# Seven products in place of eight for the first product of experts 3 to 7, with their weights through one staging buffer

## The chip, the cores and the metric

The kernel runs on one core of a Trainium2 chip. The metric is the time of one execution on the device, in microseconds (us); lower is better. The engines are PE (TensorE: matmuls, which write to PSUM, and PEld, its weight loads), DVE (VectorE), ACT (ScalarE), POOL (GpSimd) and SP (SyncE, which in the kernel before issues every DMA). Each engine runs its instructions in the order in which they stand in its queue; an instruction that waits for a semaphore holds up all that stand behind it.

## The reference

Gated linear attention makes 3072 rows of 384 values, and a mixture of eight experts works on every row with weights from a Sinkhorn iteration.

```python
# attention, batch 4, 8 heads, 768 steps, head dim 48
state = alpha[:, :, t, :, None] * state + einsum('bhd,bhe->bhde', k[:, :, t], v[:, :, t])
y[:, :, t] = einsum('bhd,bhde->bhe', q[:, :, t], state)

# experts: x [3072, 384], w_gate [384, 8], w1 [8, 384, 1024], w2 [8, 1024, 384]
P = exp(logits - logits.max())                  # logits = x @ w_gate
for _ in range(8):
    P /= P.sum(1, keepdims=True) + 1e-09
    P /= P.sum(0, keepdims=True) + 1e-09
    P *= N / E
for e in range(E):
    h = maximum(x @ w1[e], 0.0)
    out += P[:, e:e + 1] * (h @ w2[e])
```

## The kernel before, in words

Each operand of the experts' products is held as two float16 halves, high and low, and a product is made in three passes (high by high, high by low, low by high: `PASSES`). The rows come as `xT[0]` and `xT[1]`, with the 384 values in three k tiles of 128 partitions and 3072 tokens along the free axis. The weights are scaled by a power of two that comes from their largest entry, and split into `w1h` and `w2h`.

The program has three stages. In the first the attention runs, and the products of experts 0 and 1 fill TensorE between its steps (`filler`, `fill`). The second is the Sinkhorn iteration (`sinkhorn`): eight rounds in which DVE normalises rows, PE sums columns with one matmul (`pssk`), and DVE normalises columns. Between two rounds `fill(2.8)` puts about 2.8 us of the left-over products of experts 0 and 1 on PE. Up to there (`hold`) every engine's instructions stand in the order of the code. In the third stage, experts 2 to 7, PE keeps the order of the code and a scheduler places the instructions of the other engines when the program is built.

An expert is worked on in six tiles of 512 tokens (`moe_tile`). For each of eight f tiles, nine matmuls of 512 columns (three k tiles by three passes) add up in one PSUM bank. ACT then writes the relu as `h[0]`, and DVE writes what the rounding left as `h[1]`. For each of four groups of 128 tokens, 24 matmuls of 384 columns make the second product (tiles `ps2_...`), and DVE adds it to `acc` by `evac_add`. The PSUM banks come from a pool of four, `psm`; the other four belong to the attention's pools `psa` and `psb`.

`load_expert` brings the weights: one DMA of 1536 KB each for `w1f` and `w2f`, issued by SP into a pool `wst` of two buffers; three DVE maxima (`w1m`, `w2m`); a maximum over partitions on POOL (`w1g`, `w2g`); four small DVE steps (`pow2_scale`, steps m, p, r, s); and the split, ACT for the high half and DVE for the low. The split weights `wp` are double-buffered too. In the third stage one step of the next expert's load goes with every piece of this expert's products (`next(more, None)`), so that it lies all along the expert. Every instruction that a `Held` wrapper records is on line 56, every matmul on line 65.

Of the kernel before, what the change touches and what calls it, by code (L numbers as in the profile page):

```python
# [8 lines left out]
F16 = mybir.dt.float16  # L9
F32 = mybir.dt.float32  # L10
# [13 lines left out]
def tile_gla_moe(ctx: ExitStack, tc: tile.TileContext, q, k, v, alpha, wg, w1, w2, out):  # L24
# [21 lines left out]
    class Held:  # L46
        """an engine whose instructions stay in program order while hold is set"""
# [16 lines left out]
    def mm(out_, lhsT, rhs, start=True, stop=True):  # L64
        tc.keep_in_program_order(nc.tensor.matmul(out_, lhsT, rhs, start=start, stop=stop))  # L65
# [13 lines left out]
    mask = cp.tile([P, 8], F32, name="mask")          # mask[p, b] = (p // 16 == b)  # L79
# [158 lines left out]
    def attn_block(b, u, got):  # L238
        """scores inside blocks of 16 tokens; a partition is a (block, head)"""
# [67 lines left out]
        if fast:  # L307
# [111 lines left out]
    def attn_chunk(b, ch, got):  # L419
        """128 tokens; yields where its products wait for other engines"""  # L420
# [17 lines left out]
        def decayed(x, eng, tab, L, z, s):  # L438
            """the z-th halves of x's blocks of 2L, each block of 16 times its entry of tab"""
# [18 lines left out]
        # A^T [s, (h, t)], its blocks on the diagonal first  # L458
# [5 lines left out]
        # heads of one half of the partitions to a bank of their own  # L464
# [26 lines left out]
        # the scale of a token, and the token scaled  # L491
# [66 lines left out]
    w0, w1_ = (load_expert(e, None, wAB[e]) for e in range(2))  # L558
# [22 lines left out]
    def act(a):  # L581
        """a step of: the blocks of unit 1 or 2 (b), an expert's weights (w), a chunk (c), the gate (g), the experts (f)"""
# [53 lines left out]
    def sinkhorn():  # L636
# [7 lines left out]
        for it in range(N_SINKHORN):  # L644
# [11 lines left out]
            # (sum + EPS) * E / N, so that its inverse scales too  # L656
# [5 lines left out]

    ws, wn = [], []
# [10 lines left out]
    hold[0] = False  # L674

# [21 lines left out]

    for e in range(2, E):
        wn = []
        more = load_expert(e + 1, wst, wn) if e + 1 < E else iter(())  # L700
        for t0 in range(0, NT, T):
            for _ in moe_tile(e, ws, t0, T, hp2, evac_first if e == 2 else evac_add):
                next(more, None)
        ws = wn
# [28 lines left out]
```

## Time and profile before

| | us |
|---|---|
| median of 3 runs (range) | 1891.04 (1889.03 to 1895.35) |
| profiled execution, span from first to last instruction | 1885.1 |
| PE busy | 1722.3 (91%) |
| DVE busy | 893.8 (47%) |
| ACT busy | 464.4 (25%) |
| POOL busy | 346.3 (18%) |

The page gives the profiled execution its span and no other time; the median of the runs is 5.9 us above that span. Busy time of an engine is the time in which at least one of its instructions ran. Matmuls overlap, so the mean duration of one is longer than the time that it adds. "Idle before" is the time that an engine stood still before a group of instructions, with what released it.

### The profile page before, as it was taken

To read this page: it belongs to the slowest core of one execution; us is meant where nothing else is said; L and a number is where in the kernel's file an instruction comes from. 1 tells how busy PE (TensorE), PEld (TensorE's weight loads), DVE (VectorE), ACT (ScalarE), POOL (GpSimd) and SP (SyncE) were. 2 spreads that over 40 slices of the span, in tenths; PEclk is the share of its full clock that TensorE was granted. 3 is DMA by queue.
4 is the path that set the end of the run, shared out by engine and by line. 5 is a ranking of instruction groups with operands and counts; after the bars stand their busy time and mean duration, and the time that the engine had idled before them with its cause. 6 is when DMAs were issued, how large, how long until landed. Compare 5 with 4: busy or idle time off the path is not lost.

```text
span 1885.1 us, 30215 instructions
## 1 busy us (share of the span) xinstructions
PE 1722.3 (91%) x13016; PEld 1064.5 (56%) x13016; DVE 893.8 (47%) x1723; ACT 464.4 (25%) x1008; POOL 346.3 (18%) x315
## 2 busy tenths in 40 slices
PE   0556889989889899999999999999999999999999
PEld 0435767767667786455555555555555555555555
DVE  6466766666676646952352235223423332323222
ACT  2232333333323242531221112111211121211111
POOL 4435545545455520000000000000000000000000
PEclk9867899999999999999999999999999999999999
DMA  6131233333333212640010001000100000000000
GB/s 177 57 82 46 50 89 91 87 88 92 91 76 79 68 37 85 210 134 0 34 34 1 1 34 34 1 1 34 34 1 1 1 1 1 1 1 17 34 17 34
DMA packets 143125, 92.20 MB, mean 49 GB/s; under 512 B 107152, under 2 KB 132240, under 8 KB 142992
## 3 DMA queue, kind: packets, MB, share of 16 engines
q1 hardware_dynamic: 142992, 90.28, 17.4%
q8 instruction: 102, 1.67, 0.4%
q14 instruction: 31, 0.25, 0.0%
HBM read 64.79 MB, written 25.46 MB: 48 GB/s over the span
## 4 chain that ended last, share of the span: by engine, by line
PE 65%; DVE 15%; DMA 7%; issue 5%; POOL 5%; ACT 2%; SPq 1%; POOLq 0%; ACTq 0%; DVEq 0%
PE ps L65 62%; POOL tmp L56 4%; DVE AB L56 3%; DMA kt<-in_k_dram 2%; DVE tmp L56 2%; DVE qt L56 2%; DMA ri<-raw 1%; DVE h L56 1%; PE psy L65 1%; DMA qs<-qt 1%; DVE decq L56 1%; DMA DN<-ds 1%; DVE w L56 1%; SPq L56 1%; DMA w2f<-in_moe_w_dram 1%
## 5 line engine op out<-in xcount | busy, mean ns | idle before, releaser
L65 PE MATMUL ps<-xT,w 128*128 128x512 f16 (+2 forms) x4392 | 785.1, 338 | 17.0 <-DVE h L56 11.1
L65 PE MATMUL ps<-w,h 128*128 128x384 f16 x4608 | 773.6, 328 | 10.6 <-DVE h L56 10.5
L65 PEld LDWEIGHTS <-w 128*128 128x128 f16 x4392 | 429.5, 100 | 351.0 <-issue 20.2
L65 PEld LDWEIGHTS <-h 128*128 128x128 f16 x4608 | 451.7, 98 | 308.5 <-issue 10.6
L56 ACT ACTIVATE h<-ps 128x512 f16<-128x512 f32 (+2 forms) x488 | 243.3, 505 | 898.8 <-PE ps L65 898.4
L56 DVE SCALAR_TENSOR_TENSOR h<-ps,h 128x512 f16<-128x512 f32 (+2 forms) x488 | 273.9, 574 | 362.8 <-ACT h L56 362.5
L56 DVE SCALAR_TENSOR_TENSOR acc<-ps,pe,acc 128x384 f32<-128x384 f32 x144 | 88.7, 616 | 360.7 <-PE ps L65 360.7
L56 POOL TENSOR_TENSOR tmp<-qt,kt 128x768 f32<-128x768 f32 (+1 forms) x88 | 152.2, 1734 | 152.7 <-DVE AB L56 61.7
L56 DVE TENSOR_REDUCE AB<-tmp 128x16 f32<-128x768 f32 (+2 forms) x105 | 94.6, 902 | 84.0 <-POOL tmp L56 83.5
L56 POOL PARTITION_ALL_REDUCE w1g<-w1m x8 | 2.9, 357 | 533.4 <-DVE w1m L56 521.8
L56 ACT COPY A<-psl 16x128 f32<-16x128 f32 (+2 forms) x168 | 56.0, 333 | 77.8 <-PE psl L65 66.4
L65 PE MATMUL psl<-decq,deck 48*32 48x32 f32 (+1 forms) x1152 | 33.7, 218 | 43.8 <-POOL deck L56 22.0
L65 PE MATMUL psy<-vn,A 128*128 128x48 f32 x384 | 58.1, 283 | 1.8 <-POOL w L56 1.8
L65 PEld LDWEIGHTS psy<-vn,A 128*128 128x128 f32 x384 | 54.9, 209 | 2.3 <-POOL w L56 2.2
L65 PEld LDWEIGHTS psl<-decq,deck 48*32 48x32 f32 (+1 forms) x1152 | 28.6, 129 | 46.3 <-POOL deck L56 22.6
L68 PE MATMUL psk<-ident,KN 128*128 128x128 f32 x96 | 17.4, 309 | 39.0 <-POOL KN L56 30.2
L56 POOL TENSOR_TENSOR kt<-kt,al 128x384 f32<-128x384 f32 x47 | 48.5, 1031 | 11.2 <-issue 7.1
L56 POOL TENSOR_TENSOR A<-an,mask 128x1024 f32<-128x1024 f32 x24 | 47.9, 1996 | 0.0
L56 DVE TENSOR_TENSOR qt<-qt,al 128x384 f32<-128x384 f32 (+1 forms) x55 | 46.4, 844 | 0.0
L56 ACT ACTIVATE ys<-psy,s_t 128x384 f32<-128x384 f32 x24 | 14.0, 581 | 131.4 <-DVE s_t L56 113.2
L65 PE MATMUL psy<-ST,Tq 128*128 128x96 f32 x160 | 35.2, 304 | 6.6 <-DVE wgm L56 6.2
L56 ACT COPY r<-ps 128x384 f32<-128x384 f32 x48 | 23.0, 479 | 69.3 <-PE ps L65 60.1
(139 smaller groups left out, 914.6 us busy)
## 6 DMA issues: line engine op xcount, KB each, us to landing
raw<-r SPq DMA_DIRECT2D x48, 192.0 KB, 1.9
w1f<-in_moe_w_dram SPq DMA_DIRECT2D x6, 1536.0 KB, 6.7
w2f<-in_moe_w_dram SPq DMA_DIRECT2D x6, 1536.0 KB, 6.9
ri<-raw SPq DMA_DIRECT2D x48, 192.0 KB, 2.5
qt<-in_q_dram SPq DMA_DIRECT2D x12, 384.0 KB, 4.3
al<-in_alpha_dram SPq DMA_DIRECT2D x12, 384.0 KB, 5.3
kt<-in_k_dram SPq DMA_DIRECT2D x12, 384.0 KB, 6.2
KN<-ks SPq DMA_DIRECT2D x24, 192.0 KB, 3.1
```

The lines of the kernel that those rows point to most:

```text
L56: r = f(*a, **k_)
L65: tc.keep_in_program_order(nc.tensor.matmul(out_, lhsT, rhs, start=start, stop=stop))
L68: tc.keep_in_program_order(nc.tensor.transpose(out=out_, in_=in_, identity=idn))
```

## The change

For experts 3 to 7 two tiles of 512 tokens, a and b, are worked on together, and so are two f tiles, f and f+4. The first two k tiles make a 2 by 2 block product, done with seven products in place of eight (Strassen's scheme, in the form with shared sums). The third k tile is added in the plain way, by four products. A group of one f therefore has eleven products of three passes, 33 matmuls of 512 columns, where 36 stood. The sums that the scheme needs are made once for the tokens (`sums`, tiles `sx0`, `sx1`, during expert 2), and once an expert for the weights (`split_w1`, nine half-width pieces in `w1s0`, `w1s1`).

Inside a group four PSUM banks are used: A (`sta`), E (`ste`), B (`stb`) and D (`std`). A product that is part of two results is copied by ACT from bank to bank or to SBUF (`s2`, `s5`), and two DVE additions join the parts. I number the products as the code does. In its order PE makes A0, E3 | A1, A7, B4, E2, E8, B5 | D6, D7, B8, and between the second and third part of a group stand A0 and E3 of the next group, if there is one in the pair. Two dashes mark a tile of that next group (A''1).

```diff
+    def group(f):
...
+            prod(A, 0, f, X(0, ta), True)
+            SE.copy(B, A)
+            prod(E_, 3, f, S(0), True)
+            SE.copy(s5, E_)
+            yield
+            prod(A, 1, f, X(1, ta))
+            prod(A, 7, f, X(2, ta))
+            done(A, 0, f)
+            prod(B, 4, f, S(1))
+            SE.copy(s2, B)
+            prod(E_, 2, f, S(3))
+            prod(E_, 8, f, X(2, ta))
+            VE.tensor_add(E_, E_, s2)
+            done(E_, 0, f + FT // 2)
+            prod(B, 5, f, S(2))
+            SE.copy(D_, B)
+            yield
+            prod(D_, 6, f, X(1, tb))
+            prod(D_, 7, f, X(2, tb))
+            done(D_, 1, f)
+            prod(B, 8, f, X(2, tb))
+            VE.tensor_add(B, B, s5)
+            done(B, 1, f + FT // 2)
+            yield
+        groups = [group(f) for f in range(FT // 2)]
+        next(groups[0])
+        for f, g in enumerate(groups):
+            next(g)
+            yield
+            if f + 1 < len(groups):
+                next(groups[f + 1])
+            next(g)
+            yield
```

`prod` is three matmuls, `done` the relu on ACT and the remainder on DVE. The second product is as before but for the order of its f tiles (0, 1, 2, 4, 5, 6, 3, 7), eight groups of 128 tokens one after the other.

The weights are loaded in another way, for expert 2 too. The staging pool has one buffer, which `w1f` and `w2f` of all experts share in turn; the split `w1s` is single-buffered; and POOL issues the DMAs.

```diff
-    wst = ctx.enter_context(tc.tile_pool(name="wst", bufs=2))
+    wst = ctx.enter_context(tc.tile_pool(name="wst", bufs=1))
+    wsp = ctx.enter_context(tc.tile_pool(name="wsp", bufs=1))
...
+    def stage_w1(e):
+        t = wst.tile([P, KT_, FF], F32, tag="wst", name=f"w1f_{e}")
+        GE.dma_start(t, w1[e].rearrange("(c p) f -> p c f", p=P))
+        yield
...
+    def load_w2(e):
+        t = wst.tile([P, FT, DM], F32, tag="wst", name=f"w2f_{e}")
+        GE.dma_start(t, w2[e].rearrange("(c p) f -> p c f", p=P))
...
-    w2_ = load_expert(2, wst, ws)
+    w2_ = chain(stage_w1(2), split_w1(2, True), load_w2(2))
     for n, _ in enumerate(sinkhorn()):
-        advance(w2_, n < 5)
+        advance(w2_, 2)
         fill(2.8 if n else 4.0)
...
+                    else:
+                        if y == "second":
+                            late = chain(stage, split_w1(e + 1, False), load_w2(e + 1))
+                        next(late, None)
```

So the order for an expert's successor is: `w1f` is loaded and its maxima taken early; `split_w1` stands behind the last first product of the expert, since it overwrites `w1s`; the DMA of `w2f` stands behind the split, since it overwrites the staging buffer; and the DMA of the next `w1f` behind the split of `w2f`. Four plain matmuls ahead of expert 2 (`bits`) set PSUM's accumulate bits in the new banks. During expert 2 `sums` adds 14 DVE and 4 ACT instructions of 512 columns for each of three pairs.

Place 1 is PE around the end of the first products of a pair. In the kernel before, one f tile follows another with a bank of its own (`ps1_<expert>_<first token>_<f>`):

```order
L65 MATMUL ps1_4_512_6_12052<-xT1_78,w10_4_10416 128x512
L65 LDWEIGHTS w11_4_10417
L65 MATMUL ps1_4_512_6_12052<-xT0_77,w11_4_10417 128x512
L65 LDWEIGHTS w10_4_10416
L65 MATMUL ps1_4_512_7_12064<-xT0_77,w10_4_10416 128x512 [waits DVE_49]
L65 LDWEIGHTS w10_4_10416
L65 MATMUL ps1_4_512_7_12064<-xT1_78,w10_4_10416 128x512
L65 LDWEIGHTS w11_4_10417
L65 MATMUL ps1_4_512_7_12064<-xT0_77,w11_4_10417 128x512
```

Now, in the last group of a pair, product 6 in bank D (`std`) follows product 5 in bank B (`stb`):

```order
L65 MATMUL stb_4_1_3_12501<-sx0_8868,w1s0_4_11623 128x512 [waits Activation_49]
L65 LDWEIGHTS w1s0_4_11623
L65 MATMUL stb_4_1_3_12501<-sx1_8869,w1s0_4_11623 128x512
L65 LDWEIGHTS w1s1_4_11624
L65 MATMUL stb_4_1_3_12501<-sx0_8868,w1s1_4_11624 128x512
L65 LDWEIGHTS w1s0_4_11623 [waits DVE_49]
L65 MATMUL std_4_1_3_12502<-xT0_80,w1s0_4_11623 128x512 [waits Activation_49]
L65 LDWEIGHTS w1s0_4_11623
L65 MATMUL std_4_1_3_12502<-xT1_81,w1s0_4_11623 128x512
L65 LDWEIGHTS w1s1_4_11624
L65 MATMUL std_4_1_3_12502<-xT0_80,w1s1_4_11624 128x512
```

No other product stands between the two, and the first matmul on `std` waits for ACT, whose row for it copies `stb` to `std`.

Place 2 is DVE in the first round of the Sinkhorn iteration, from the row normalisation (`PR`, `ri`) to the column sums (`cs`). Before:

```order
L56 TENSOR_TENSOR PR_8393<-PR_8393,ri_0_8404 128x192 [waits DVE_49]
L56 SCALAR_TENSOR_TENSOR h1_0_2816_8356<-ps1_0_2816_2_8411,h0_0_2816_8355 128x256 [waits Activation_49]
L56 SCALAR_TENSOR_TENSOR h1_0_2816_8356<-ps1_0_2816_3_8423,h0_0_2816_8355 128x256 [waits Activation_49]
L56 SCALAR_TENSOR_TENSOR h1_0_2816_8356<-ps1_0_2816_4_8435,h0_0_2816_8355 128x256 [waits Activation_49]
L56 SCALAR_TENSOR_TENSOR h1_0_2816_8356<-ps1_0_2816_5_8447,h0_0_2816_8355 128x256 [waits Activation_49]
L56 SCALAR_TENSOR_TENSOR h1_0_2816_8356<-ps1_0_2816_6_8459,h0_0_2816_8355 128x256 [waits Activation_49]
L56 TENSOR_REDUCE cs_0_8473<-pssk_0_8471 128x8 [waits PE_49]
```

And now, with `w1m_2`, the first maximum over the load of expert 2, between the two:

```order
L56 TENSOR_TENSOR PR_8396<-PR_8396,ri_0_8407 128x192 [waits DVE_49]
L56 TENSOR_REDUCE w1m_2_8412<-w1f_2_8410 128x1 [waits DMAHW4_49,DMAHW3_49,DMAHW7_49,DMAHW0_49,DMASW0_49]
L56 SCALAR_TENSOR_TENSOR h1_0_2816_8359<-ps1_0_2816_2_8414,h0_0_2816_8358 128x256 [waits Activation_49]
L56 SCALAR_TENSOR_TENSOR h1_0_2816_8359<-ps1_0_2816_3_8426,h0_0_2816_8358 128x256 [waits Activation_49]
L56 SCALAR_TENSOR_TENSOR h1_0_2816_8359<-ps1_0_2816_4_8438,h0_0_2816_8358 128x256 [waits Activation_49]
L56 SCALAR_TENSOR_TENSOR h1_0_2816_8359<-ps1_0_2816_5_8450,h0_0_2816_8358 128x256 [waits Activation_49]
L56 SCALAR_TENSOR_TENSOR h1_0_2816_8359<-ps1_0_2816_6_8462,h0_0_2816_8358 128x256 [waits Activation_49]
L56 TENSOR_REDUCE cs_0_8476<-pssk_0_8474 128x8 [waits PE_49]
```

The maximum waits for a DMA and stands ahead of five remainders `h1`, which free PSUM banks, and of the column sums.

Place 3 is DVE at the end of expert 3, around the last second products. Before, with the maxima over `w1f_6` and the split `w21_5` among the last `acc` of expert 3 and the first `h1` of expert 4:

```order
L56 TENSOR_REDUCE w1m_6_13074<-w1f_6_13044 128x1
L56 TENSOR_TENSOR pe_4_2_11947<-PR_8393,wsc_81 128x1 [waits DVE_49]
L56 TENSOR_REDUCE w1m_6_13074<-w1f_6_13044 128x1
L56 TENSOR_REDUCE w1m1_6_13102<-w1m_6_13074 128x1 [waits DVE_49]
L56 TENSOR_SCALAR m_w1_6_13118<-w1g_6_13104 128x1 [waits Pool_49]
L56 TENSOR_SCALAR p_w1_6_13120<-m_w1_6_13118 128x1 [waits DVE_49]
L56 TENSOR_SCALAR r_w1_6_13122<-p_w1_6_13120 128x1 [waits DVE_49]
L56 SCALAR_TENSOR_TENSOR acc_8392<-ps2_3_2560_3_11687,pe_3_23_11712,acc_8392 128x384 [waits PE_49]
L56 TENSOR_SCALAR s_w1_6_13124<-r_w1_6_13122 128x1 [waits DVE_49]
L56 TENSOR_TENSOR pe_4_3_11975<-PR_8393,wsc_81 128x1 [waits DVE_49]
L56 SCALAR_TENSOR_TENSOR w21_5_11746<-w2f_5_11747,s_w2_5_11885,w20_5_11745 128x1152 [waits Activation_49] x2
L56 SCALAR_TENSOR_TENSOR h1_4_0_11716<-ps1_4_0_0_11717,h0_4_0_11715 128x512 [waits Activation_49]
```

And now, where `w1m_5` are the maxima over the first weights of expert 5 and `ste_4_0_0` is the first addition of expert 4; the split `w21_4` of expert 4's second weights stands three rows ahead of the first row:

```order
L56 SCALAR_TENSOR_TENSOR acc_8395<-ps2_3_2_1_2_11844,pe_3_22_11869,acc_8395 128x384 [waits PE_49]
L56 TENSOR_TENSOR pe_4_2_12197<-PR_8396,wsc_84 128x1 [waits DVE_49]
L56 TENSOR_REDUCE w1m_5_12413<-w1f_5_12383 128x1 [waits DMASW6_49]
L56 SCALAR_TENSOR_TENSOR acc_8395<-ps2_3_2_1_3_11872,pe_3_23_11897,acc_8395 128x384 [waits PE_49]
L56 TENSOR_REDUCE w1m_5_12413<-w1f_5_12383 128x1
L56 TENSOR_TENSOR pe_4_3_12225<-PR_8396,wsc_84 128x1 [waits DVE_49]
L56 TENSOR_REDUCE w1m_5_12413<-w1f_5_12383 128x1
L56 SCALAR_TENSOR_TENSOR h1_4_0_0_11901<-sta_4_0_0_11904,h0_4_0_0_11900 128x512 [waits Activation_49]
L56 TENSOR_REDUCE w1m1_5_12495<-w1m_5_12413 128x1 [waits DVE_49]
L56 TENSOR_TENSOR wx_5_13016<-w1f_5_12383 128x512
L56 TENSOR_TENSOR ste_4_0_0_11905<-ste_4_0_0_11905,s2_4_0_0_11908 128x512 [waits PE_49,Activation_49]
```

Before, these maxima belong to the next but one expert and a buffer of their own; now they wait for a DMA whose room the split of `w2f_4` frees, and stand ahead of the last `acc` and of the first addition.

More of the change, by code (lines that the diff above doesn't have):

```diff
@@ L62, in tile_gla_moe, with mm @@
     VE, SE, GE, SP = (Held(x) for x in (nc.vector, nc.scalar, nc.gpsimd, nc.sync))
-    def mm(out_, lhsT, rhs, start=True, stop=True):
-        tc.keep_in_program_order(nc.tensor.matmul(out_, lhsT, rhs, start=start, stop=stop))
+    def mm(out_, lhsT, rhs, start=True, stop=True, **k_):
+        tc.keep_in_program_order(nc.tensor.matmul(out_, lhsT, rhs, start=start, stop=stop, **k_))
     def tr(out_, in_, idn):
@@ L557, in tile_gla_moe @@
     wAB = [[], []]
-    w0, w1_ = (load_expert(e, None, wAB[e]) for e in range(2))
+    w0, w1_ = (load_expert(e, wAB[e]) for e in range(2))
     wgf = cp.tile([P, KT_, E], F32, name="wgf")
@@ new lines, in split_w1, with put @@
+    def split_w1(e, plain):
+        t, pw, sc = pw1[e]
+        hl = w1s[e] = [wsp.tile([P, 9, HF], F16, tag=f"w1s{i}", name=f"w1s{i}_{e}") for i in range(2)]
+        q = lambda c, z: t[:, c, z * HF:(z + 1) * HF]
+        def put(n, src, m=1):
+            o = [x[:, n:n + m].rearrange("p n w -> p (n w)") for x in hl]
+            split(src, sc, *o)
+        if plain:
+            for c in range(KT_):
+                put(2 * c, t[:, c], 2)
+                yield
+            return
+        x = wst.tile([P, HF], F32, tag="wx", name=f"wx_{e}")
+        b12 = q(0, 1)
+        put(0, q(0, 0))
+        VE.tensor_sub(x, b12, q(0, 0))
+        yield
+        VE.tensor_sub(b12, q(1, 1), b12)
+        put(5, b12)
+        yield
+        put(3, x)
+        VE.tensor_sub(b12, q(1, 1), x)
+        yield
+        put(4, b12)
+        VE.tensor_sub(x, q(1, 0), b12)
+        yield
+        put(1, q(1, 0))
+        yield
+        put(2, q(1, 1))
+        put(6, x)
+        yield
+        put(7, t[:, 2], 2)
+        yield
@@ L665, in tile_gla_moe, with chain @@
+    def chain(*gens):
+        for g in gens:
+            yield from g
+    w2_ = chain(stage_w1(2), split_w1(2, True), load_w2(2))
     for n, _ in enumerate(sinkhorn()):
-        advance(w2_, n < 5)
+        advance(w2_, 2)
         fill(2.8 if n else 4.0)
@@ L674, in tile_gla_moe @@
     hold[0] = False
+    early.close()
+    attn_ps.close()
     T = 512
@@ L696, in evac_add @@
             SP.dma_start(out[tt * P:(tt + 1) * P], acc[:, tt])
-    for e in range(2, E):
[L699 to L704, printed above, removed]
+    hp2 = ctx.enter_context(tc.tile_pool(name="hp2", bufs=2, side="right"))
+    sp = ctx.enter_context(tc.tile_pool(name="sp", bufs=2, side="right"))
@@ new lines, in tile_gla_moe, with sums, put @@
+    pss_ = ctx.enter_context(tc.tile_pool(name="pss_", bufs=4, space=PSUM))
+    sx = [wsp.tile([P, 4, NT // 2], F16, tag=f"sx{i}", name=f"sx{i}") for i in range(2)]
+    def sums(b):
+        ta, tb, to = (slice(x, x + T) for x in (2 * b * T, (2 * b + 1) * T, b * T))
+        a11, a12, a21, a22 = ([x[:, c, t] for x in xT] for t in (ta, tb) for c in range(2))
+        f = [sp.tile([P, T], F32, tag=f"sf{i}", bufs=1, name=f"sf{i}_{b}") for i in range(2)]
+        def put(n, s):
+            SE.copy(sx[0][:, n, to], s)
+            VE.tensor_sub(sx[1][:, n, to], s, sx[0][:, n, to])
+        s1, s3 = f
+        VE.tensor_add(s1, a21[0], a22[0])
+        VE.tensor_add(s1, s1, a21[1])
+        VE.tensor_add(s1, s1, a22[1])
+        put(0, s1)
+        yield
+        VE.tensor_sub(s3, a11[0], a21[0])
+        VE.tensor_add(s3, s3, a11[1])
+        VE.tensor_sub(s3, s3, a21[1])
+        put(2, s3)
+        yield
+        VE.tensor_sub(s1, s1, a11[0])
+        VE.tensor_sub(s1, s1, a11[1])
+        put(1, s1)
+        yield
+        VE.tensor_sub(s3, a12[0], s1)
+        VE.tensor_add(s3, s3, a12[1])
+        put(3, s3)
+        yield
@@ new lines, in tile_gla_moe @@
+    for n in range(4):
+        mm(pss_.tile([P, T], F32, tag="pss", name=f"bits{n}"), ident.bitcast(F16)[:, :P], xT[0][:, 0, :T])
+    for e in range(2, E):
+        nxt = e + 1 < E
+        stage = stage_w1(e + 1) if nxt else iter(())
+        if e == 2:
+            extra = chain(*(sums(b) for b in range(NT // T // 2)))
+            ws = [[x[:, :6].rearrange("p (c z) w -> p c (z w)", z=2) for x in w1s[2]], w2s[2]]
+            for t0 in range(0, NT, T):
+                for n, _ in enumerate(moe_tile(e, ws, t0, T, hp2, evac_first)):
+                    if n < FT:
+                        if n % 2:
+                            next(extra, None)
+                    elif t0 < NT - T:
+                        next(stage, None)
+                    else:
+                        if n == FT:
+                            late = chain(stage, split_w1(e + 1, False), load_w2(e + 1))
+                        next(late, None)
+                        next(late, None)
+        else:
+            for b in range(NT // T // 2):
+                last = nxt and b == NT // T // 2 - 1
+                second = False
+                if b == 1:
+                    advance(late, 99)
+                for y in strassen(e, b, evac_add):
+                    second = second or y == "second"
+                    if b == 0:
+                        next(late, None)
+                    elif not (second and last):
+                        next(stage, None)
+                    else:
+                        if y == "second":
+                            late = chain(stage, split_w1(e + 1, False), load_w2(e + 1))
+                        next(late, None)
```

93 lines of the change are left out of this document (75 added, 18 removed).

## The prediction

> **What bounds the kernel now.** The page first: how busy each engine is, where in the span, and which engine the chain that ended last runs through.
>
> ```profile
> span 1885.1 us, 30215 instructions
> PE 1722.3 (91%) x13016; PEld 1064.5 (56%) x13016; DVE 893.8 (47%) x1723; ACT 464.4 (25%) x1008; POOL 346.3 (18%) x315
> PE   0556889989889899999999999999999999999999
> PE 65%; DVE 15%; DMA 7%; issue 5%; POOL 5%; ACT 2%; SPq 1%; POOLq 0%; ACTq 0%; DVEq 0%
> ```
>
> PE is the bound, and from the 19th slice on it never rests. Then the windows: the last 900 us, the Sinkhorn rounds, the load of expert 2's weights behind them, and a stretch of the attention right after PE had stood still.
>
> ```profile
> core 0: us, PE busy (x) PEld busy (x) DVE busy (x) ACT busy (x) POOL busy (x), PEclk, DMA share, GB/s
> 985.00:1885.00 900.00, 896.28 (x4841) 473.45 (x4839) 284.15 (x510) 155.43 (x247) 1.40 (x4) 1.00 0.04 13
> 720.40:750.10 29.70, 27.36 (x199) 19.74 (x196) 25.30 (x79) 6.48 (x17) 0.73 (x2) 1.00 0.07 24
> 750.10:808.20 58.10, 55.94 (x294) 28.32 (x293) 53.73 (x117) 28.52 (x41) 1.40 (x4) 1.00 0.58 191
> 487.80:497.80 10.00, 9.86 (x121) 8.46 (x121) 8.65 (x17) 4.53 (x13) 4.35 (x4) 0.83 0.03 9
> ```
>
> From 985 us PE is busy 99.6% at full clock, with DVE at 32% and ACT at 17%: a matmul saved there is time saved, and a wait of PE is time lost one for one. In the Sinkhorn rounds DVE has only 29.7 - 25.3 = 4.4 us to spare. The page's time is a span of 1885.1; the median of the runs is 5.9 above, and I add my sum to the median.
>
> **The change: what it removes.** The last groups by shape (mean duration, which overlaps) and a stretch of the timeline give the real price of a matmul and of the two steps behind a product.
>
> ```profile
> L65 PE MATMUL ps<-xT,w 128*128 128x512 f16 x2016 | 439.7, 379 | 0.0
> L56 DVE SCALAR_TENSOR_TENSOR h<-ps,h 128x512 f16<-128x512 f32 x224 | 154.6, 691 | 269.8 <-ACT h L56 269.8
> L56 ACT ACTIVATE h<-ps 128x512 f16<-128x512 f32 x224 | 133.6, 597 | 679.8 <-PE ps L65 679.8
> 1102.62 15.70 PE L65 MATMUL ps<-xT,w 128*128 128x512 f16 x72
> 1104.76 0.60 ACT L56 ACTIVATE h<-ps 128x512 f16<-128x512 f32 x1 [16.95 <-PE ps L65]
> 1105.39 0.69 DVE L56 SCALAR_TENSOR_TENSOR h<-ps,h 128x512 f16<-128x512 f32 x1 [1.76 <-ACT h L56]
> 1106.70 0.60 ACT L56 ACTIVATE h<-ps 128x512 f16<-128x512 f32 x1 [1.34 <-PE ps L65]
> ```
>
> Two relus are 1.94 us apart, which is nine matmuls: 0.2157 us each, a product of three 0.647. The first relu starts 2.14 after the start of the 72, which is 0.20 after the ninth matmul's end: that is PE to ACT; ACT to DVE is 0.03. A group now has 33 matmuls where 36 stood, and there are 5 experts of 3 pairs of 4 groups: 60 x 3 = 180 matmuls go, 180 x 0.2157 = -38.8. The four `bits` add 4 x 0.2157 = +0.9.
>
> **The last group of a pair.** Product D6 there stands right behind B5 and starts from a copy of B by ACT. The copy's price is that of the same shape in the attention; the way from DVE to PE (a first remainder of 0.42 from 722.78 ends at 723.20, PE starts at 723.25) is 0.05.
>
> ```profile
> L56 ACT COPY Tq<-psq 128x512 f32<-128x512 f32 x24 | 14.3, 596 | 0.4 <-PE psq L68 0.3
> 722.78 1.41 DVE L56 SCALAR_TENSOR_TENSOR h<-ps,h 128x256 f16<-128x256 f32 x4
> 723.25 1.14 PE L65 MATMUL ps<-xT,w 128*128 128x256 f16 x9 [0.19 <-DVE h L56]
> ```
>
> PE waits 0.20 + 0.60 + 0.05 = 0.85, 15 times: +12.8. A copy of 0.4 or 0.9 us would give 9.8 or 17.3; I take the row, which has this shape. In the first group of a pair A1 goes on in bank A, which ACT must have copied to B before: the same 0.85 against the one product, E3 (0.647), that lies between leaves 0.20, 15 times: +3.0 (0 to 0.4 each, so 0 to 6). In the other groups the next group's A''0 and E''3 lie in that place. There ACT and DVE work a chain from the end of B8: relu D 0.20 + 0.60, remainder 0.69, addition 0.68 (an addition has no row of that shape; I take the remainder's), relu B 0.60, then 0.5 of the next relu; 3.27 against the five products, 3.235, that PE has before it wants the bank. That is level, so +2 (0 to 45 x 0.3 = 13).
>
> **Sinkhorn.** `w1f_2` was issued by SP at 710.24. Now POOL issues it, and its queue holds the all-reduce of `gg` ahead of it.
>
> ```profile
> 710.24 0.38 SPq L56 DMA_DIRECT2D w1f<-in_moe_w_dram  x1
> 720.40 0.38 POOL L56 PARTITION_ALL_REDUCE gg<-gm  x1 [15.22 <-DVE gm L56]
> 722.50 0.36 DVE L56 TENSOR_TENSOR PR<-PR,ri 128x192 f32<-128x192 f32 x1
> w1f<-in_moe_w_dram SPq DMA_DIRECT2D x6, 1536.0 KB, 6.7
> w2f<-in_moe_w_dram SPq DMA_DIRECT2D x6, 1536.0 KB, 6.9
> qt<-in_q_dram SPq DMA_DIRECT2D x12, 384.0 KB, 4.3
> xT<-in_moe_w_dram SPq DMA_DIRECT2D x2, 384.0 KB, 8.7
> ```
>
> Issued at 720.8 and landed 6.7 to 7 later, at about 727.7, while the first maximum stands on DVE right behind `PR` of 722.5, ahead of the remainders and the column sums. DVE stands from 722.9 to 727.7, and what it did then waits: 4.8 and the maximum's own 1.2, 6.0. No run shows a load issued by POOL, so the landing is bounded by rows of SP, 4.3 for a quarter of the bytes and 8.7, the longest here; I take 6.8, the rows with the same bytes. The steps `advance(w2_, 2)` now put more of the load's work among the rounds:
>
> ```profile
> L56 DVE SCALAR_TENSOR_TENSOR w<-w1f,s_w,w 128x1024 f16<-128x1024 f32 x18 | 22.5, 1280 | 7.7 <-ACT w L56 7.6
> L56 DVE TENSOR_REDUCE w1m<-w1f 128x1 f32<-128x1024 f32 x18 | 21.8, 1212 | 10.5 <-DMA w1f<-in_moe_w_dram 10.5
> L56 DVE SCALAR_TENSOR_TENSOR w<-w2f,s_w,w 128x768 f16<-128x768 f32 x6 | 6.1, 1009 | 0.0
> L56 DVE TENSOR_REDUCE w2m<-w2f 128x1 f32<-128x768 f32 x6 | 5.7, 942 | 0.0
> L56 ACT ACTIVATE w<-w2f,s_w 128x768 f16<-128x768 f32 x6 | 5.5, 922 | 0.0
> ```
>
> Added there: three splits of 1.28, four maxima of 0.94, one split of 1.01 and two further steps of about 1.3, 11.2 in all. The load of `w2f` waits for the split of `w1f` (one buffer), lands 7 later, and some 3.3 of DVE's other work lies beside that: 3.7 more of standing. 6.0 + 11.2 + 3.7 = 20.9, less the 4.4 that DVE had free: +16 (11 to 22). PE has work for 27.4 us in these rounds and cannot fill more. Behind them, at 750 to 808, DVE is relieved of that work, but PE was busy 55.94 of 58.1 there, so at most 2.2 comes back; I count 0. The `sums` lie beside expert 2's products, on a DVE that is busy a third of the time.
>
> **From expert 2 to 3.** I walk from T0, the end of expert 2's last first product, behind which the split of the next `w1` may start. DVE's share of that split is seven remainders of 0.69, one of 1.28, four subtractions (the nearest row, 384 columns, 0.55) and three or four additions to `acc` between, together 10.7. The shapes, and the steps behind the maxima (an all-reduce, then small ones):
>
> ```profile
> L56 DVE SCALAR_TENSOR_TENSOR acc<-ps,pe,acc 128x384 f32<-128x384 f32 x144 | 88.7, 616 | 360.7 <-PE ps L65 360.7
> L56 DVE TENSOR_TENSOR xT<-psx,xT 128x384 f16<-128x384 f32 x24 | 13.1, 546 | 4.5 <-ACT xT L56 4.5
> 773.87 0.15 DVE L56 TENSOR_REDUCE w1m<-w1m 128x1 f32<-128x3 f32 x1
> 774.11 0.35 POOL L56 PARTITION_ALL_REDUCE w1g<-w1m  x1 [12.06 <-DVE w1m L56]
> 774.53 0.14 DVE L56 TENSOR_SCALAR m_w<-w1g 128x1 f32<-128x1 f32 x1
> L65 PE MATMUL ps<-w,h 128*128 128x384 f16 x2746 | 451.0, 326 | 0.0
> ```
>
> Then 6.9 for `w2f` (17.6), four maxima (21.4), all-reduce, four small steps and an addition, 2.6 (24.0), four ACT splits of 0.92, which stand ahead of relu E and the copy of D (27.7), and those two (28.9). PE wants that copy after the rest of the second product, 96 matmuls of 384 columns at 451.0/2746 = 0.164, which is 15.75 from T0, plus 0.2 and ten products of 0.647: 22.4. It waits 6.5, and about 1.0 more in the next group, whose s2 copy is late: +7.5 (0 to 11).
>
> **From 3 to 4, 4 to 5, 5 to 6.** Here, after the same 10.4 + 6.9 + 3.8 + 2.7 + 4.7 (the last is the split of `w2f`, until the last remainder has read it) = 28.5, POOL issues the next `w1f`, which lands at 35.3; DVE stands at its maximum, which is ahead of the addition of the last `ps2` tile and of the first addition to E. Maximum at 36.5, `acc` at 37.1. The second product of these lasts 31.5 from T0 (192 matmuls), and PE wants the bank that `acc` frees at 31.5 + 0.2 + 9 x 0.647 = 37.5: just in time. But two more maxima, a remainder, two steps and the addition to E, 5.9 in all, stand ahead of the B'' copy: done at 43.0 against 31.5 + 0.2 + 13 x 0.647 = 40.1. With about 1.0 for the late s2, 4.0 each: +12 (0 to 24). At 6 to 7 there is no next `w1f`, so nothing. All of this goes if both landings take 4.7 us or less.
>
> The Trainium skill, page "DMA: Bandwidth & Descriptors", section "Anatomy of one DMA — SWDGE (gpsimd) path", gives a load issued by POOL 2.0 us and its bytes over 436 GB/s: for these 1,572,864 bytes an estimate of 5.6, less than the 6.7 and 6.9 that SP's rows show. By it the rounds would cost 2.6 less, the step 2 to 3 1.3 less and the three others 2.6 each less, and the sum would end near 1898; no run here shows a load by POOL yet, and the sum goes by the rows.
>
> **The clock.** After PE stood 2.47 us for its clock was lower for a while:
>
> ```profile
> 487.74 1.76 PE L65 MATMUL psl<-decq,deck 48*32 48x32 f32 x48 [2.47 <-DVE deck L56]
> ```
>
> The next 10 us ran at 0.83, so 1.7 us were lost. The change has one long wait in the first round, one or two more in the others and one at 2 to 3: +4 (0 to 10).
>
> Sum: -38.8 + 0.9 + 12.8 + 3.0 + 2 + 16 + 7.5 + 12 + 4 = +19.4, and 1891 + 19 = 1910.
>
> **Rivals.** *The load is covered (faster).* If DVE never stands at a maximum, because the loads land well before it gets there, the 6.0 - 1.2 and 3.7 of the rounds, the 7.5, the 12 and the clock's 4 go: 32, and the time is 1878. For it speaks that the DMA engines are free (share 0.04 in the last 900 us); against it, that the issue, and not the landing, is late by the order of POOL's queue and by the single buffer. It decides where the landings fall under about 3 us, or where the first load's issue gets past the all-reduce of `gg` by those 6 us.
> *About the same.* Landings of 4.7 or less hide the later steps, but not the rounds: without 7.5, 12, 4 less 1, that is 1888.
> *Slower still.* In the 45 other groups ACT and DVE, not PE, set the pace: 0.3 more each, 13 in place of 2, and with PE stopping that often the clock costs its full 10 in place of 4: 1910 + 11 + 6 = 1927. For it speaks the walk above, which came out level; against it, 155 us of ACT and 284 of DVE in 900.
>
> **How the numbers follow.** A change of under 0.3% (5.7 us) can't be told from none: 1885.4 to 1896.7 is the same. Chances: my sum 0.62, covered 0.18, same 0.11, slower still 0.09. Within my sum's own range, 1895 to 1925, one part in ten falls below 1896.7. So faster 0.19, same 0.16, slower 0.65. The range reaches down towards the covered case and up to the slowest: 1880 to 1931.
>
> **What the changed profile would show.** The 180 matmuls: 12,840 in place of 13,016, and and a wait of PE for the copy to `std` of 0.85, fifteen times. In the first round: a maximum of DVE that waits near 4.8 us for the load, rounds of 46 in place of 29.7 us. At 2 to 3, PE waits for ACT's copy of D by 6.5; at the three next steps DVE waits at `w1m` for the load, then PE at the B'' copy by about 3. It would be wrong if POOL's loads land in 5 us or 9, if the copy in PSUM costs other than 0.60, or if a group's chain runs over.

## The result, and the profile after

| | before | after |
|---|---|---|
| median of 4 runs, us | 1890.07 | 1913.89 (1909.81 to 1918.0) |
| profiled span, us | 1885.1 | 1908.1 |

The ratio is 1.0119, 95% interval 1.0095 to 1.0142: 1.2% slower, 23.8 us by the medians and 23.0 us by the two profiled spans. The forecast was 1910, 19 us slower, in a range of 1880 to 1931. The sum was close, but one of its parts had the wrong stage: some two fifths of the loss lie where I had looked for none.

Three windows show this: up to the all-reduce `gg`, from there to the start of expert 3's first product, and the rest. First the kernel before, with its first matmul of expert 3 at 946.92, then the changed kernel, where that is 973.5. The columns are those of the prediction's windows; behind each window stands its length.

```profile
0.00:720.40 720.40, 567.84 (x6744) 450.58 (x6745) 456.70 (x857) 234.92 (x641) 341.73 (x303) 0.93 0.33 84
720.40:946.92 226.52, 220.13 (x1236) 120.85 (x1234) 133.94 (x319) 64.43 (x106) 2.48 (x7) 1.00 0.25 82
946.92:1885.10 938.18, 934.36 (x5041) 493.07 (x5039) 303.19 (x548) 165.10 (x261) 2.10 (x6) 1.00 0.04 14
```

```profile
0.00:730.20 730.20, 564.87 (x6743) 448.79 (x6744) 457.42 (x857) 234.56 (x641) 341.86 (x302) 0.93 0.35 79
730.20:973.50 243.30, 223.88 (x1239) 123.48 (x1237) 141.92 (x334) 67.65 (x118) 5.09 (x8) 0.97 0.22 68
973.50:1908.10 934.60, 906.20 (x4862) 476.42 (x4859) 416.62 (x751) 298.83 (x532) 10.94 (x17) 0.99 0.06 20
```

The attention takes 9.8 us more (forecast: nothing), Sinkhorn and expert 2 16.8 more (forecast: 16 and 0.9 for `bits`), and experts 3 to 7 3.6 less (forecast, without the clock's 4: 1.5 less). The matmul count fell by 176 as said, to 12,840.

The attention's instructions and their order are the same in both kernels. The chief wait that grew there is one of PE for a small DMA, `DN`. From the waits up to 720 us (total, times, longest), before:

```profile
PE psd L68 <- DMA DN<-ds: 19.3, 8, 9.0
```

and after:

```profile
PE psd L68 <- DMA DN<-ds: 29.2, 9, 10.2
```

The DMA issues of the changed kernel (median from issue to landing at the end):

```profile
w1f<-in_moe_w_dram POOLq DMA_DIRECT2D x6, 1536.0 KB, 7.0
w2f<-in_moe_w_dram POOLq DMA_DIRECT2D x6, 1536.0 KB, 7.5
...
KN<-ks SPq DMA_DIRECT2D x24, 192.0 KB, 3.7
...
DN<-ds SPq DMA_DIRECT2D x12, 24.0 KB, 3.6
```

Before, `KN` landed in 3.1 us and `DN` in 2.5:

```profile
KN<-ks SPq DMA_DIRECT2D x24, 192.0 KB, 3.1
...
DN<-ds SPq DMA_DIRECT2D x12, 24.0 KB, 2.5
```

In the rounds the two waits for loads that I forecast are there. From the timeline of the changed kernel:

```profile
731.01 1.06 POOL L56 DMA_DIRECT2D w1f<-in_moe_w_dram  x1 [0.41 <-PE ps L65]
...
738.09 1.22 DVE L56 TENSOR_REDUCE w1m<-w1f 128x1 f32<-128x1024 f32 x1 [5.33 <-DMA w1f<-in_moe_w_dram]
...
739.70 2.08 PE L65 MATMUL ps<-xT,w 128*128 128x256 f16 x9 [6.82 <-DVE h L56]
...
767.48 1.81 DVE L56 TENSOR_REDUCE w2m<-w2f 128x1 f32<-128x768 f32 x2 [4.47 <-DMA w2f<-in_moe_w_dram]
...
769.67 4.00 PE L65 MATMUL ps<-xT,w 128*128 128x256 f16 x18 [4.97 <-DVE h L56]
```

DVE stood 5.3 us at the first maximum (forecast 4.8) and 4.5 at the second (3.7); behind each, PE stood for banks that DVE's remainders free. The rounds, from `gg` to the last column sums, took 50.9 us (forecast 46, before 29.7), with 214 matmuls in place of 199:

```profile
730.20:781.06 50.86, 33.63 (x214) 23.23 (x212) 34.63 (x96) 11.61 (x23) 3.06 (x5) 0.87 0.20 70
```

From there to expert 3 the changed kernel takes 192.4 us where the one before took 196.8. So the rounds lost 21.2, and 4.4 came back behind them.

For experts 3 to 7 the waits of PE (from 950 us on), and one end of a pair in the timeline:

```profile
PE std L65 <- ACT std L56: 15.2, 16, 5.3
PE sta L65 <- ACT stb L56: 7.6, 3, 2.6
PE ste L65 <- DVE acc L56: 1.5, 1, 1.5
PE stb L65 <- ACT s L56: 0.5, 1, 0.5
```

```profile
1041.84 0.81 PE L65 MATMUL ste<-sx,w1s 128*128 128x512 f16 x3
1042.66 1.46 PE L65 MATMUL sta<-xT,w1s 128*128 128x512 f16 x6
...
1067.26 0.81 PE L65 MATMUL stb<-sx,w1s 128*128 128x512 f16 x3
1068.73 1.46 PE L65 MATMUL std<-xT,w1s 128*128 128x512 f16 x6 [0.66 <-ACT std L56]
```

A lesson in reading: a product lasts 0.647 from start to start, but its row says 0.81, since the modelled end of a matmul lies past the next one's start. So the idle time of a row is too small by 0.16. From start to start D6 waits 1.47 - 0.65 = 0.82 (forecast 0.85), and A1, whose row shows no wait, 0.82 - 0.65 = 0.17 (forecast 0.20).

### The profile page after: what moved, and what is told of

Read it like the earlier page. It is cut to its first block, busy times and chain, and to the rows that moved or that the text cites. A ratio compares the mean times of both kernels' runs of the same rounds, so it can differ in the third digit from the quotient of the medians.

```text
span 1908.1 us, 30544 instructions
## 1 busy us (share of the span) xinstructions
PE 1694.9 (89%) x12840; PEld 1048.7 (55%) x12840; DVE 1016.0 (53%) x1942; ACT 601.0 (31%) x1291; POOL 357.9 (19%) x327
## 4 chain that ended last, share of the span: by engine, by line
PE 48%; DVE 4%; DMA 2%; ACT 1%; issue 1%; POOL 0%; POOLq 0%; ACTq 0%; DVEq 0%
PE ps L65 27%; PE stb L65 6%; PE sta L65 6%; PE ste L65 6%; PE std L65 4%; DMA ri<-raw 1%; DMA w2f<-in_moe_w_dram 1%; DMA w1f<-in_moe_w_dram 1%; DVE acc L56 1%; DVE w1s L56 1%; ACT std L56 0%; DVE h L56 0%; DVE w L56 0%; DVE w2m L56 0%; DVE sf L56 0%
## 5 line engine op out<-in xcount | busy, mean ns | idle before, releaser
L65 PEld LDWEIGHTS <-w1s 128*128 128x128 f16 x2412 | 237.0, 98 | 318.5 <-issue 43.3
L65 PE MATMUL ps<-xT,w 128*128 128x256 f16 (+1 forms) x1800 | 218.2, 279 | 28.9 <-DVE h L56 24.0
L65 PEld LDWEIGHTS <-w 128*128 128x128 f16 x1800 | 175.4, 102 | 59.3 <-issue 32.4
L56 ACT ACTIVATE h<-ps 128x256 f16<-128x256 f32 (+2 forms) x248 | 99.6, 417 | 199.3 <-PE ps L65 198.7
L56 DVE SCALAR_TENSOR_TENSOR h<-ps,h 128x256 f16<-128x256 f32 (+2 forms) x248 | 108.6, 461 | 81.1 <-ACT h L56 80.8
L65 PE MATMUL sta<-xT,w1s 128*128 128x512 f16 x540 | 136.5, 380 | 7.7 <-ACT stb L56 7.6
L65 PE MATMUL std<-xT,w1s 128*128 128x512 f16 x360 | 88.7, 383 | 15.2 <-ACT std L56 15.2
L65 PE MATMUL ste<-sx,w1s 128*128 128x512 f16 x360 | 98.6, 383 | 1.5 <-DVE acc L56 1.5
L65 PE MATMUL stb<-sx,w1s 128*128 128x512 f16 x360 | 98.6, 383 | 0.5 <-ACT s L56 0.5
L65 PE MATMUL ps<-xT,w1s 128*128 128x512 f16 x432 | 94.4, 379 | 1.3 <-DVE h L56 1.3
```

The lines of the kernel that those rows point to most:

```text
L56: r = f(*a, **k_)
```

## The experiments

My theory after this: the losses from the rounds on are those of my walk, and the attention's 9.8 come from something that the change did to SP's small reads. Two candidates for the latter: POOL's software queue, which is new in the program (theory A), or the buffers' places in SBUF, which the changed pools moved (theory B).

**Loads by SP** (`sp_loads`).

```diff
-        GE.dma_start(t, w1[e].rearrange("(c p) f -> p c f", p=P))
+        SP.dma_start(t, w1[e].rearrange("(c p) f -> p c f", p=P))
...
-        GE.dma_start(t, w2[e].rearrange("(c p) f -> p c f", p=P))
+        SP.dma_start(t, w2[e].rearrange("(c p) f -> p c f", p=P))
```

> The changed kernel, with the twelve loads of weights issued by SP again and nothing else changed. Theory A (POOL's software queue, by being in the program, makes SP's small reads of DRAM in the attention about 1.1 us slower): the load DN lands in 2.5 us again, the first all-reduce gg stands near 720 in place of 730 us, and the first maximum of the rounds no longer waits 5.3 us, since SP issues the load without waiting for gg. That is 9.8 + 5.3 less than 1914: about 1898. Theory B (the new pools moved the buffers in SBUF, and that makes these reads slower): DN stays near 3.6 and gg near 730, and only the 5.3 goes: about 1908.

Measured 1897.26 (ratio to the kernel before 1.0038, 1.0025 to 1.0051). The time is theory A's, the trace is not: `gg` stands at 733.4, and `DN` lands in 3.5 us. A falls, and what is gained lies elsewhere: 7.6 between `gg` and expert 3, where SP issues the load at 723.25, ten us ahead of `gg`, and 8.0 in experts 3 to 7, of which my expectation had nothing. (`gg` comes 3.2 later than in the profile of the changed kernel, so the profiled spans are 12.4 apart, the medians 16.6.) From its waits after 950 us, and its DMA rows:

```profile
PE sta L65 <- ACT stb L56: 2.4, 3, 0.9
```

```profile
w1f<-in_moe_w_dram SPq DMA_DIRECT2D x6, 1536.0 KB, 6.3
w2f<-in_moe_w_dram SPq DMA_DIRECT2D x6, 1536.0 KB, 7.0
```

The waits at the B'' copy shrink from 7.6 to 2.4. Two loads in a row land 0.7 and 0.5 earlier than POOL's, 1.2 together, and they are issued earlier: at the end of expert 4 SP's `w2f` starts 0.05 us behind the last remainder of the split, POOL's 0.56. So the first maximum over `w1f` starts 2.3 earlier there, and the wait at each B'' copy is 1.7 shorter. Another 3.2 of the 8.0 is the clock, which no longer falls behind these waits (see the point on the clock below).

**One store by POOL** (`one_pool_store`), in the kernel before.

```diff
-            SP.dma_start(out[tt * P:(tt + 1) * P], acc[:, tt])
+            (GE if tt == 0 else SP).dma_start(out[tt * P:(tt + 1) * P], acc[:, tt])
```

> The kernel before, with one of its 24 stores of the output (the first tile of the last expert, at the very end) issued by POOL in place of SP. Theory A: one software transfer anywhere in the program is enough, gg moves from 720 to 730 and the time from 1890 to about 1900, though the transfer itself comes 1000 us later. Theory B: nothing moves, 1890.

Measured 1891.7 (1.0004, 0.9991 to 1.0017), `DN` 2.5, `gg` at 721.8: nothing moves. That POOL's software queue is in the program does not slow SP's reads; whether loads by POOL at the same time would, no run shows.

**128 bytes of padding**, in both kernels (`before_shift`, `after_shift`). In the program that is built, the tiles `QN`, `KN` and `DN` start at 64 past a multiple of 512 bytes in the kernel before (`DN` at 145472) and at 192 in the changed one (104640), since `wp1` and `hp1` went to the other side of SBUF. Their DMAs write pieces of 192 bytes (48 values), 256 apart.

```diff
     warm = cp.tile([P, 1], F32, name="warm")
+    pad = cp.tile([P, 32], F32, name="pad")
+    VE.memset(pad, 0.0)
```

> The kernel before, with an unused tile of 128 bytes a partition ahead of the attention's buffers, so that all of these lie 128 bytes further in SBUF (the tiles KN, QN and DN start at 192 past a multiple of 512 bytes in place of 64, as they do in the changed kernel). Theory: SP's reads of DRAM are written in pieces of 192 bytes, 256 apart, and where a piece lies across a boundary of 256 or 512 bytes in SBUF, landing takes longer; then DN takes 3.6 in place of 2.5 us, gg stands near 730 and the time is about 1900. Rival: the place as such (40 KB lower in the changed kernel) or something else of its pools makes the difference: DN 2.5, time 1890.

> The changed kernel with the same unused 128 bytes, which put KN, QN and DN at 320 past a multiple of 512 bytes (64 past one of 256) in place of 192. Theory of the boundary: DN lands in 2.5 us again, gg stands near 720, the time is about 1904. Rival, the place as such: 1914.

Measured: the kernel before becomes slower, 1901.39 (1.0064, 1.0044 to 1.0084), with `gg` at 735.6; the changed kernel becomes faster, 1900.67 (1.0060, 1.0041 to 1.0079, against 1.0119 without the padding), with `gg` at 717.8. The rows of the DMA issues, of the kernel before with padding and then of the changed kernel with it:

```profile
KN<-ks SPq DMA_DIRECT2D x24, 192.0 KB, 3.6
...
DN<-ds SPq DMA_DIRECT2D x12, 24.0 KB, 3.5
```

```profile
KN<-ks SPq DMA_DIRECT2D x24, 192.0 KB, 3.1
...
DN<-ds SPq DMA_DIRECT2D x12, 24.0 KB, 2.5
```

The same 128 bytes cost the one what they gave the other: 1.0 to 1.1 us per landing of `DN`, and 11 to 13 us of time. `QN` moves with them, 3.2 to 4.3 us in the one and 4.4 to 3.2 in the other. Theory B is shown, in the form that where the pieces start decides, not how far up in SBUF the buffer lies. How much each load loses by its own pieces is not separated: SP issues these loads one right behind the other, and `an`, which follows them with pieces of 64 bytes that cross no multiple of 256 in either place, lands 1.2 later too (4.2 in place of 3.0).

**Which starts** (`before_pad64`, `before_pad192`, `before_pad224`): the same tile with 16, 48 and 56 values in place of 32, one run each.

> The kernel before with 64 unused bytes ahead: KN, QN and DN start at 128 past a multiple of 512, their pieces of 192 bytes at 128 and 384, so that each lies across a boundary of 256 or 512 (128 to 320, 384 to 576). Theory of the boundary: DN 3.5 us and gg near 730 or later. Rival: only the offset 192 is bad, or every odd multiple of 64 but one: DN 2.5, gg near 721.

> The kernel before with 192 unused bytes ahead: the pieces start at 256 and 0 past a multiple of 512 and end at 448 and 192, across nothing. Theory of the boundary: DN 2.5 us, gg near 721. Rival, any shift from the first place costs: DN 3.5, gg near 730.

> The kernel before with 224 unused bytes ahead: the pieces start at 288 and 32 past a multiple of 512 and end at 480 and 224, across no boundary of 256, but at no multiple of 64. Theory of the boundary: DN 2.5 us, gg near 721. Rival, that starts have to be multiples of 64 as well: DN longer than 2.5.

| pieces start at, past a multiple of 256 | end at | `DN`, median us | `gg` at, us |
|---|---|---|---|
| 64 (before) | 256 | 2.5 | 720.4 |
| 0 (192 bytes) | 192 | 2.6 | 721.2 |
| 32 (224 bytes) | 224 | 2.6 | 722.9 |
| 128 (64 bytes) | 320 | 3.6 | 738.1 |
| 192 (128 bytes) | 384 | 3.5 | 735.6 |

Where the pieces stay inside 256 bytes `DN` lands fast, also from a start that is no multiple of 64; where they lie across a boundary it lands 1 us later. (The times of these single runs, in the order 64, 192 and 224 bytes, are 1904.78, 1886.98 and 1890.75, beside one run of 1896.27 of the kernel before; the landings are the clearer witness.) All thirteen profiles of this case fall in the same two groups: `DN` at 2.5 to 2.6 with `gg` at 717.8 to 722.9, or `DN` at 3.5 to 3.6 with `gg` at 729.3 to 738.1. The Trainium skill, page "DMA: Bandwidth & Descriptors", section "How a descriptor splits into AXI transactions", says that a descriptor is cut at multiples of 256 bytes, and that one that starts off such a multiple begins with the boundary below. By it a piece from 64 to 256 is one transaction and one from 192 to 384 two. These five rows agree with that; the page tells it of reading, here it is the side that is written in SBUF that was moved.

**E8 between B5 and D6** (`d6_later`), in the changed kernel.

```diff
             prod(A, 1, f, X(1, ta))
+            prod(B, 4, f, S(1))
+            SE.copy(s2, B)
             prod(A, 7, f, X(2, ta))
             done(A, 0, f)
-            prod(B, 4, f, S(1))
-            SE.copy(s2, B)
             prod(E_, 2, f, S(3))
+            prod(B, 5, f, S(2))
+            SE.copy(D_, B)
             prod(E_, 8, f, X(2, ta))
             VE.tensor_add(E_, E_, s2)
             done(E_, 0, f + FT // 2)
-            prod(B, 5, f, S(2))
-            SE.copy(D_, B)
```

> The changed kernel, with the order of products in a group changed to A1, B4, A7, E2, B5, E8, so that E8 stands between B5 and D6. Theory: what D6 waits for in the last group of a pair is the copy of B alone, 0.82 us between starts beyond a product; with a product of 0.65 in between 0.17 is left, 15 times 0.65 = 9.8 less, about 1904. Rival: relu A and the addition to E come 0.65 later, and ACT's and DVE's chain in a group, which came out level with PE by my walk, gives that back in the 45 other groups: 1914 or more.

Measured 1907.19 (1.0084, 1.0058 to 1.011). Of the sixteen waits at `std` one is left; the period of a pair falls from 60.68 to 60.22, 15 x 0.455 = 6.8 of the 9.8. (The three waits at the B'' copies are still there, 2.3 each, now at B5.) The rest is the rival's, as ACT and PE show in the timeline:

```profile
1048.84 0.60 ACT L56 ACTIVATE h<-stb 128x512 f16<-128x512 f32 x1 [1.36 <-DVE stb L56]
1049.21 0.81 PE L65 MATMUL ste<-sx,w1s 128*128 128x512 f16 x3
1049.34 0.58 ACT L56 COPY s<-stb 128x512 f32<-128x512 f32 x1
1049.97 0.81 PE L65 MATMUL stb<-sx,w1s 128*128 128x512 f16 x3
```

The `s2` copy now stands behind the relu of the last group's B, and B5 starts 0.76 behind E2 in place of 0.65; in the next two groups 0.69 and 0.70.

**Second weights first** (`w2_first`), in the changed kernel. The split of the first weights is then the only step behind the last first product.

```diff
-        stage = stage_w1(e + 1) if nxt else iter(())
+        stage = chain(load_w2(e + 1), stage_w1(e + 1)) if nxt else iter(())
...
-                            late = chain(stage, split_w1(e + 1, False), load_w2(e + 1))
+                            late = chain(stage, split_w1(e + 1, False))
...
-                if b == 1:
+                if b == 0:
                     advance(late, 99)
```

(The factor `wsc` is then made in two steps, and three empty steps stand behind each load.)

> The changed kernel, with the next expert's second weights loaded and split ahead of its first weights, so that behind the last first product of an expert only the split of w1 is left, and no load. Theory: PE's waits at the ends of experts 2 to 5 (5.5 at the copy of D, 8.0 in three waits and 2.3 around them, by the gaps between matmuls) all come from the two loads in a row through one buffer, and go with the clock's loss behind them, about 4.5: 20 less, about 1894. Rival: the split of w1 itself, 10 us of DVE and ACT, holds PE as well, and half stays: about 1904. Second rival: the maxima now wait for their loads inside a pair, on DVE, and PE waits there instead: 1914.

Measured 1899.49 (1.0051, 1.0028 to 1.0074), 14.4 less; from expert 3 on 920.4 in place of 934.6. Theory in the main, 5 us short of its 1894. The first rival falls: the split of `w1` is done at 969.6, before PE starts expert 3 at 976.2. Its waits after 950 us:

```profile
PE std L65 <- ACT std L56: 11.8, 16, 1.9
PE stb L65 <- ACT s L56: 2.7, 5, 0.6
PE sta L65 <- ACT stb L56: 0.6, 3, 0.2
```

The second rival has the rest: the load of expert 4's `w2f` starts right behind the split, the scheduler puts its maxima ahead of the next work on DVE, and DVE stands there, though PE waits for less of it:

```profile
970.12 0.92 POOL L56 DMA_DIRECT2D w2f<-in_moe_w_dram  x1 [142.16 <-issue]
...
977.88 1.81 DVE L56 TENSOR_REDUCE w2m<-w2f 128x1 f32<-128x768 f32 x2 [4.60 <-DMA w2f<-in_moe_w_dram]
...
984.92 1.46 PE L65 MATMUL std<-xT,w1s 128*128 128x512 f16 x6 [1.94 <-ACT std L56]
```

**One step a round** (`slow_rounds`), in the changed kernel.

```diff
-        advance(w2_, 2)
+        advance(w2_, n < 5)
```

> The changed kernel, with the load of expert 2's weights advanced by one step in each of the first five Sinkhorn rounds, as in the kernel before, in place of two in all rounds; the rest of it then lies among and behind the left-over products. Theory: the rounds hold 11 us of splits and maxima on DVE that the kernel before did later, under PE's products, and by the lines of the trace some 9 us of PE's standing hang on them (4.97 at a remainder, and seven waits of 0.2 to 1.6 at the column sums); they go, but expert 2's first products then wait for the split of w1: between 3 and 9 less, about 1908. Rival: the work is only moved and PE waits as long for it at the start of expert 2: 1914.

Measured 1899.44 (1.0048, 1.0032 to 1.0064), 14.5 less, above what I gave it. POOL still issues the load behind `gg`, but the first maximum now stands in the second round:

```profile
730.09 1.06 POOL L56 DMA_DIRECT2D w1f<-in_moe_w_dram  x1 [0.41 <-PE ps L65]
...
737.11 1.22 DVE L56 TENSOR_REDUCE w1m<-w1f 128x1 f32<-128x1024 f32 x1 [0.42 <-DMA w1f<-in_moe_w_dram]
```

It waits 0.42 us. From `gg` to expert 3 are 230.2 us (243.3 with two steps, 226.5 before), so the pace is worth 13 of the 16.8 lost there, POOL's late issue with it. My expectation had left the first wait out, since I held it for POOL's alone.

**All together** (`all_shift`): loads by SP, second weights first, E8 between, one step a round, and the padding.

> The changed kernel with all of it together: loads issued by SP, second weights first, E8 between B5 and D6, one step a round, and the 128 bytes. By the single runs, against 1914: SP's issue 7.4 in the rounds, second weights first 14.2, E8 between 15 x 0.65 = 9.8, the 128 bytes 9.8, the steps 3 to 9: 44 to 50 less, about 1867, which is 24 less than the kernel before. If the gains overlap (the loads by SP hold up the reads of the first experts' rows in SP's queue, or the two orders meet at the ends of the experts), 1875 to 1885.

Measured 1865.16 (0.9878, 0.9863 to 0.9893): 1.2% faster than the kernel before. In its windows all three stages are near or below those of before:

```profile
0.00:722.60 722.60, 571.03 (x6743) 452.46 (x6744) 457.27 (x858) 234.62 (x641) 341.80 (x302) 0.92 0.33 82
722.60:950.70 228.10, 221.51 (x1239) 121.07 (x1238) 149.22 (x352) 71.19 (x122) 2.09 (x5) 1.00 0.24 73
950.70:1863.00 912.30, 905.07 (x4862) 475.39 (x4859) 413.04 (x738) 298.59 (x528) 3.68 (x8) 1.00 0.05 18
```

From expert 3 on 912.3 stand against 938.2: 25.9 of the 38.8 that 180 matmuls are worth now arrive. The rest is, from start to start of the matmuls, 3.2 at A1, 3.2 at B5, 5.2 at D6 (2.7 of it once, behind expert 2) and 1.7 of lower clock, some 13 together.

## Why the prediction was right, point by point

- **The sign and the size** held, 1913.9 against 1910, partly by luck: 9.8 us were missing (the attention), and the terms behind it were 6.2 too high together (19.4 against 13.2).
- **The last group's copy**, +12.8: measured 15 x 0.82 = 12.3, and `d6_later` left 0.17 of each. **A1**, +3.0: 15 x 0.17 = 2.6. **The other groups**, +2: nothing shows in the changed kernel; that the margin was as thin as my walk said, two things show: there the copy to `s2` mostly ends only 0.10 to 0.16 before B5 starts, and `d6_later` has its 0.04 to 0.11 a group.
- **Sinkhorn and `bits`**, +16.9: measured 16.8, and that these meet is luck: the rounds grew by 21.2 where I had 16, and 4.4 came back behind them where I counted 0 and at most 2.2. The mechanism was half named: I gave the first wait to POOL's queue, and it takes POOL's queue and the two steps a round; SP's issue alone gave back 7.6, the pace alone 13.
- **Expert 2 to 3**, +7.5: measured 5.3 and 0.2 of the modelled end; the 1.0 that I had added for the next group is not there. From T0 at 957.9 the copy of D was done 27.7 us later, where I had 28.9, and PE wanted it at 980.3, the 22.4 of the forecast: the load took 1.0 more than I gave it, the split 1.1 less and the steps behind the load 1.1 less. From the timeline:

```profile
967.48 0.92 POOL L56 DMA_DIRECT2D w2f<-in_moe_w_dram  x1 [164.08 <-issue]
...
975.41 3.53 DVE L56 TENSOR_REDUCE w2m<-w2f 128x1 f32<-128x768 f32 x4 [4.97 <-DMA w2f<-in_moe_w_dram]
...
985.66 2.72 PE L65 MATMUL std<-xT,w1s 128*128 128x512 f16 x6 [5.33 <-ACT std L56]
```

- **The three next ends**, +12: measured 7.6 at the B'' copies (three, where forecast), 1.5 at `acc`, 0.5 at `s2`, and 0.16 more each, 10.4. `w2_first` shows that both come from the two loads through one buffer. POOL's loads took 7.0 and 7.5 us, above the 6.8 that I took. The Trainium skill, page "DMA: Bandwidth & Descriptors", section "Anatomy of one DMA — SWDGE (gpsimd) path", gives 2.0 us and the bytes over 436 GB/s, by which I had estimated 5.6; the measurement decides, and the sum by that page, 1898, was further off.
- **The clock**, +4: too small, and in part in the wrong place. I had put it in the rounds and behind the wait at 2 to 3. From expert 3 on the waits and the matmuls explain -38.8 + 12.3 + 2.6 + 5.5 + 10.4 = -8.0, measured are -3.6. The 4.4 left are the clock's: it stood at 0.50 for 3.4 us behind the wait at 2 to 3 and again at two of the three next ends (from 1176.5 and from 1548.5), for which I had counted nothing. There a product takes 1.28 from start to start (1178.35 - 1177.07) in place of 0.647, and 23 matmuls lose 4.7 together. Behind the wait of 2.6 at the end of expert 4 the clock stayed full. In the rounds it stood at 0.50 twice, for 6.8 us each; the matmuls there took some 3.5 longer, which lies inside the 21.2.

```profile
736.10:742.90 6.80, 3.21 (x15) 2.30 (x15) 3.22 (x7) 0.38 (x1) 0.00 (x0) 0.50 0.19 78
766.90:773.70 6.80, 4.03 (x19) 2.96 (x19) 5.98 (x15) 0.38 (x1) 0.00 (x0) 0.50 0.00 0
985.30:988.70 3.40, 3.04 (x8) 1.11 (x8) 1.31 (x2) 1.53 (x4) 0.76 (x1) 0.50 0.35 39
1176.50:1179.90 3.40, 3.40 (x10) 1.22 (x8) 2.56 (x4) 1.56 (x3) 0.00 (x0) 0.50 0.00 0
```

```profile
1177.07 1.49 PE L65 MATMUL stb<-sx,w1s 128*128 128x512 f16 x3
1178.35 1.49 PE L65 MATMUL ste<-sx,w1s 128*128 128x512 f16 x3
```

- **What was missing**: I costed the attention at nothing, since its instructions and their order do not change. The diff moved two pools to the other side of SBUF, and I did not ask what that does to the addresses of buffers that it does not name.

## What to carry to other kernels

A saving on the bound engine is gross: list what the saved instructions had covered, here a copy between banks, a load through one buffer and the steps of a load among serial rounds, and price each by a walk from row to row; in the stages that I walked the sum came within a few us, in the rounds only because two errors met. The scheme was worth its matmuls only once these were mended, and each was a few lines: the order of the two loads, the pace of the steps, a product between a copy and its reader. When pools change, compare the addresses of all tiles that small DMAs write to, also of those that the change doesn't touch.

## What the hardware showed

- SP's reads of DRAM, written to SBUF in pieces of 192 bytes, land later when the pieces lie across a multiple of 256 bytes: `DN` in 3.5 to 3.6 us in place of 2.5 to 2.6, `KN` in 3.6 to 3.7 in place of 3.1 to 3.3, the loads ahead of each in SP's queue included. The attention reads `DN` once in each of its twelve units, `KN` and `QN` twice; by the place of `gg` that is 10 to 18 us against the kernel before.
- A load of 1536 KB issued by POOL landed in 7.0 (`w1f`) and 7.5 us (`w2f`) in the changed kernel, issued by SP in the same program in 6.3 and 7.0. Over all programs here `w2f` takes 7.3 to 7.8 by POOL and 6.7 to 7.0 by SP; for `w1f` the two overlap. The issue of one keeps POOL busy for 0.8 to 1.1 us.
- Behind most of PE's waits of 2.5 us and more in experts 2 to 7 of the changed kernel and behind two of 5 and 7 us in the rounds, the granted clock stood at 0.50 for 3.4 or 6.8 us, and matmuls took twice as long from start to start; behind the waits of 1.1 and less of `sp_loads` and of 2.1 of `w2_first`, from expert 3 on, it did not fall.
